# Conversion turns moved from the last batch to batches 2 to 6, and a last V stage with its additions ahead of its statistics

## The chip, the cores and the metric

The kernel runs on one core of a Trainium2 chip. Such a core has engines that run side by side, each with its own queue of instructions: TensorE (PE in the profile, with its weight loader PEld), VectorE (DVE), ScalarE (ACT), GpSimd (POOL) and SyncE (SP), which here issues the DMAs. The metric is the device time of one execution in microseconds. Several runs give a median; one execution was also recorded by the profiler.

## The reference

The program chains three blocks over 8 batches of 576 rows and 512 columns. All sums are kept at float32 accuracy.

```python
# 1. linear attention, 8 heads of 64
q_s = softmax(q, axis=-1); k_s = softmax(k, axis=2)
kv = einsum('bhsd,bhse->bhde', k_s, v)
x = einsum('bhsd,bhde->bhse', q_s, kv)          # then heads side by side: 576 x 512
# 2. gated MLP
h = gelu_tanh(x @ w_in); u, v = h[..., :512], h[..., 512:]
v_n = (v - mean(v)) / sqrt(var(v) + 1e-6) * g_ln
v_s = einsum('ts,bsd->btd', w_sg, v_n) + b_sg[None, :, None]
x = x + (u * v_s) @ w_out
# 3. token mix of rank 32, then channel MLP
u = x + (x.transpose(0, 2, 1) @ U @ V).transpose(0, 2, 1)
out = u + maximum(u @ w_ch1, 0) @ w_ch2         # w_ch1 512 x 2048, w_ch2 2048 x 512
```

## The kernel before

A number is kept as a high and a low part, and a product is three matmuls (high by high, low by high, high by low; `prod`). A tile is 128 rows, so a batch has four tiles of rows and a rest of 64; they are numbered t = 0 to 4.

**Stages of a batch.** The work is a loop over eight batches, numbered 1 to 8 here (0 to 7 in the code). Of each batch the loop runs the V stage (`emit_Vh`: products `pv`, GELU into `ge` on ACT; `stats`: statistics `bst`, `mv` on DVE; `emit_ln`: shift `sh` on DVE, evaluation on ACT, high part `vh` and low part `vl`), then the U stage (`emit_Uh`: products `pu`), the S stage (`emit_S`: products `pS` over the rows, gate `gt` on DVE; `split_G`: `gh` on ACT, `gl` on DVE) and the output stage (`emit_y`: products `py`, addition of `x` into `yt` on DVE). In the last three stages the attention of the next batch runs beside them, and after the output stage `emit_xT` computes that batch's x, transposed: products `px`, copies `xh` and `x` on ACT, low part `xl` on DVE. The first matmuls of the next V stage read `xl`.

**The token mix** of a batch runs inside the next batch's V stage: `emit_yT` transposes (`pt`, then `yh` on ACT and `yl` on DVE), `emit_U` gives `pp` and `pst`, and `emit_PV` gives `pw`, which DVE adds to `yt`; SP then stores `yt` into a buffer in DRAM. `pw`, `pu`, `pS` and `py` share banks, so a product waits until DVE has read the one that had its bank. After batch 8 comes the channel MLP, a Strassen-Winograd scheme of seven products over factors `wd` of the two weight matrices, first in seven steps beside batch 8's token mix, then in groups of steps. Its matmuls are `mm` and `pm`, its weights are loaded as `wu<-wd`.

**Conversion.** Both channel weights arrive as 64-bit floats. A block of them is loaded into `stg`, clamped on POOL (line 171), its exponent is made on ACT (line 177, `f<-stg`), and the fraction is merged in on DVE (lines 183 and 184). Factors are sums of blocks (`f<-f,f`), split into a high part on ACT (`chw<-f`, line 61) and a low part on POOL or DVE (`chw<-f,chw`, line 55), and stored as `wd`. The work is cut into turns. A cycle of eleven turns makes four blocks and seven factors. `turn` begins one item and carries earlier ones a stage on: start after 1 turn, merge after 3, high part after 4, low part after 5, store after 6.

**What sets the order.** PE and DVE carry out the loop in the order in which the program writes it; on ACT, POOL and SP a scheduler orders the instructions of the loop. The places of the turns are written in the table `TURNS[b][stage]`, whose stages are V, U, S, output, and the x products of the next batch. An entry is one slot: `slot` does a turn for each T, and for other letters a single earlier item (P, W, B, S: a split, a store, a bound, a start). `DVE_FACTOR_LOWS` and `DVE_FACTOR_SUMS` say which factors of a batch have low parts and additions on DVE. `STEP_TURNS` and `GROUP_TURNS` do the same for the seven steps and the groups. The slots of the output stage stand ahead of `emit_y` in all batches but the first, where the slot of the first product stands behind it. Most instructions are recorded with the line of a helper: `mm` is line 52, `tt` line 55, `copy` line 61.

Of the kernel before, what the change touches and what calls it, by code (L numbers as in the profile page):

```python
# [22 lines left out]
def fused_kernel(tc, q, k, v, w_in, g_ln, w_sgT, b_sg, w_out, U, V, w_ch1, w_ch2, outT):  # L23
    nc = tc.nc
    B, S, C = q.shape
    P = 128
    H, D = 8, 64
    NT = S // P
# [20 lines left out]
    pe, act, dve, pool, sp = nc.tensor, nc.scalar, nc.vector, nc.gpsimd, nc.sync  # L49
# [421 lines left out]
    def q_max(b, t):  # L471
        if t == 0:
            q_s[b] = tmpp.tile([P, NT + 1, H], F32, tag="qm", name="qm")
        dve.tensor_reduce(
            out=q_s[b][0 : TR[t], t], in_=q3(t), op=ALU.max, axis=mybir.AxisListType.X
        )
# [95 lines left out]
    def behind(eng):  # L572
        return tc.issue_after(last[eng].ins)
# [35 lines left out]
    def emit_Vh(b, t):  # L609
        xh, xl, xr, _ = x_t[b]  # L610
        if b and t == NT:
            pv = ps1.tile([P, F], F32, tag="ps1", name="pv")
        else:
            pv = ps2.tile([P, 1024], F32, tag="big", name="pv")[:, 0:F]
        wv_h, wv_l = wi[1]
        for kc in range(NC):
            if t < NT:
                a, l = xh[:, kc, t * P : (t + 1) * P], xl[:, kc, t * P : (t + 1) * P]
                mm(pv, a, wv_h[:, kc], kc == 0, False)
                mm(pv, a, wv_l[:, kc], False, False)  # L620
                mm(pv, l, wv_h[:, kc], False, kc == NC - 1)
            else:
                a = xr[:, kc].rearrange("p j r -> p (j r)")
                mm(pv, a, wv_h[:, kc], kc == 0, False)
                mm(pv, a, wv_l[:, kc], False, kc == NC - 1)
        if b == 0 and t > 2:
            ge = as_f32(stgp.tile([P, 2, CW], F32R, tag="chw", name="ge", bufs=4)).rearrange("p j n -> p (j n)")
        elif b == B - 1 and t == NT:
            ge = tmpp.tile([P, S], F32, tag="gt", name="ge")[:, 0:F]
        else:  # L630
            ge = tmpp.tile([P, F], F32, tag="ge", name="ge", bufs=3)
        ln[b, t] = ge
        if t < NT:
            act.activation(ge, pv, AF.Gelu_apprx_tanh)
        else:
            copy(ge[0:R], pv[64 : 64 + R])
            tt(dve, ge[0:R], pv[0:R], ge[0:R], ALU.add)
            act.activation(ge[0:R], ge[0:R], AF.Gelu_apprx_tanh)

    def stats(b, t):  # L640
        ge, n = ln[b, t], TR[t]
        bst = tmpp.tile([P, 6], F32, tag="bst", name="bst", bufs=3)
        mv = tmpp.tile([P, 2], F32, tag="mv", name="mv", bufs=3)
        dve.bn_stats(out=bst[0:n], in_=ge[0:n])  # L644
        dve.bn_aggr(out=mv[0:n], in_=bst[0:n])
        dve.tensor_scalar(out=mv[0:n, 1:2], in0=mv[0:n, 1:2], scalar1=1e-6, scalar2=None, op0=ALU.add)
        tt(pool, mv[0:n, 1:2], mv[0:n, 1:2], half[0:n], ALU.pow)
        ln[b, t] = (ge, mv)
# [25 lines left out]
    def emit_ln(b, t):  # L674
        ln_scale(b, t)
        ln_split(b, t)
# [57 lines left out]
    def emit_yT(b, t):  # L734
        n = TR[t]
        if t not in ((2, 3) if b < B - 1 else (1, 2, 3)):
            pt = ps1.tile([P, C], F32, tag="ps1", name="pt1")
        else:
            pt = ps2.tile([P, 1024], F32, tag="big", name="pt1")[:, 0:C]
        for c in range(NC):  # L740
            pe.transpose(pt[0:n, c * P : (c + 1) * P], y_t[b][:, c, t * P : t * P + n], ident)  # L741
        h = wrk.tile([P, C], F32R, tag=f"vh{t}", name=f"yh{t}")
        if t < NT:
            l = wrk.tile([P, C], F32R, tag=f"vl{t}", name=f"yl{t}")
            copy(h, pt)
            low(dve, l, pt, h)
            yn[b, t] = (h, l)
        else:
            copy(h[0:R], pt[0:R])
            low(dve, h[64 : 64 + R], pt[0:R], h[0:R])  # L750
            yn[b, t] = (h,)
# [5 lines left out]
    def emit_U(b, t):  # L757
        if t == 0:
            pu_t[b] = ps1.tile([P, C], F32, tag="ps1", name="pp")
        parts = yn.pop((b, t))  # L760
        w = u_w[:, t].rearrange("p a r -> p (a r)")
        for i, y in enumerate(parts):
            mm(pu_t[b], w, y, t == 0 and i == 0, t == NT and i == len(parts) - 1)
        if t == NT:
            pp = pu_t.pop(b)
            if b < B - 1:
                s = tmpp.tile([P, S], F32R, tag="gt", name="pst")[:, 0:C]
            else:
                s = wrk.tile([P, C], F32R, tag="xr", name="pst")
            copy(s, pp)  # L770
            low(dve, s[3 * RK : P], pp[3 * RK : P], s[3 * RK : P])
            pu_t[b] = s
# [10 lines left out]
    def emit_PV(b, c):  # L783
        s = pu_t[b][:, c * P : (c + 1) * P]
        pw = ps2.tile([P, 2, 512], F32, tag="big", name="pw")
        for j in range(2):
            mm(pw[:, j, 0:HS], s, v_w[:, j * HS : (j + 1) * HS], True, True)
        y = y_t[b][:, c]
        tt(dve, two(y), halves(pw), two(y), ALU.add)
        sp.dma_start(u2d[:, c, :, b * HS : (b + 1) * HS].rearrange("j p n -> p j n"), two(y))  # L790
# [378 lines left out]
    def slot(s):  # L1169
        if isinstance(s, int):  # L1170
            more(s)
            return
        for ch in s:
            if ch == "T":
                more(1)
            elif not gate and at[0] > 0:
                if ch == "L":
                    load_ahead()
                elif {"B": at[0] + 3, "S": at[0] + 1, "M": at[0], "H": at[0], "P": idx["H"] - 1, "W": idx["P"] - 1}[ch] >= idx[ch]:
                    op(ch)  # L1180
# [35 lines left out]
    def in_order(*engines):  # L1216
# [6 lines left out]
    OPS = 4  # L1223
    TURNS = (
# [8 lines left out]
    )  # L1233
    AHEAD = 2
    STEP_TURNS = ('TT', 'TT', 'TT', 'T', 'TTT', 'TTT', 'TTT')
# [16 lines left out]
    FOLDS = ((0, 1, 2, 1, 0), (0, 0, 2, 2, 0))  # L1252
# [71 lines left out]
    for b in range(B):  # L1324
# [10 lines left out]
            fold = k_fold(nxt)  # L1335
        if b > 0:
            load_ahead()
        for t in range(NT + 1):
            emit_Vh(b, t)
            if nxt:  # L1340
                with behind(dve):
                    for t2 in Q_MAX[b > 0][t]:
                        q_max(nxt, t2)
                    for _ in range(FOLDS[b > 0][t]):
                        next(fold)
            if t < NT:
                stats(b, t)
            slot(TURNS[b][0][t])
            if t > 0:
                emit_ln(b, t - 1)  # L1350
            if t == NT:
                stats(b, t)
            if b > 0:
                for t2 in ((2,), (3, 4), (), (), ())[t]:
                    emit_yT(b - 1, t2)
            if t == 2 and b > 0:
                for t2 in range(NT + 1):
                    emit_U(b - 1, t2)
            if b > 0:
                for c in ((), (), (), (0, 1), (2, 3))[t]:  # L1360
                    emit_PV(b - 1, c)

        spread_at = 2 if b else 3
        if nxt:
# [106 lines left out]
        for c in range(NC):  # L1471
            if not nxt:
                for _ in range((3, 3, 2, 0)[c]):
                    next(prep, None)
            if b or c:
                with tc.issue_after(last['s'].ins) if not nxt and c == 0 else contextlib.nullcontext():
                    slot(TURNS[b][3][c])
            emit_y(b, c)
            if b == 0 and c == 0:
                slot(TURNS[b][3][c])  # L1480
            if nxt and 0 < c < 3:
                emit_qT(nxt, 1 + c)
                if c == 2 and b + 2 < B:
                    load_q(b + 2)
# [133 lines left out]
```

## Time and profile before

| | |
|---|---|
| median of 3 runs | 1292.64 us (1290.99 to 1294.96) |
| profiled execution | 1292.16 us |
| its span | 1290.4 us |
| mean granted TensorE clock | 0.989 |
| instructions | 20684 |
| PE busy | 1261.8 us (98%) |
| DVE busy | 969.8 us (75%) |
| ACT busy | 653.3 us (51%) |
| POOL busy | 324.3 us (25%) |
| DMA | 274.17 MB, mean 212 GB/s |

Busy shares are means over the whole span. The span has three parts: some 90 us of preparation with the first batch's attention, the loop to about 613 us, and the channel MLP. Where TensorE is busy nearly all the time, its waits are short and have to be read one by one: by the list of waits, which gives for each kind of instruction what ended its idle time, and by the timeline, whose rows give start, duration, engine, line, operation, tiles and in brackets the idle time ahead with what ended it. A row with x2 stands for two instructions.

### The profile page before, as it was taken

How to read it: one execution, taken by the hardware profiler on the slowest of the kernel's cores; microseconds unless marked ns; L12 is line 12 of the kernel's file. 1: busy time of each engine (PE TensorE's matmuls, PEld its weight loads, DVE VectorE, ACT ScalarE, POOL GpSimd, SP SyncE). 2: the span in 40 equal slices, each digit the busy share in tenths (PEclk: the TensorE clock that was granted, in tenths of full speed). 3: DMA queues.
4: the chain of work that ended last, by engine and by line, in shares of the span. 5: the costliest groups of instructions: out<-in, count | busy, mean ns of one | idle time of the engine just before them, and what ended most of it. 6: DMA issues, size and time to landing. Idle time of an engine off the chain costs nothing.

```text
span 1290.4 us, 20684 instructions
## 1 busy us (share of the span) xinstructions
PE 1261.8 (98%) x7628; PEld 1142.8 (89%) x7628; DVE 969.8 (75%) x1406; ACT 653.3 (51%) x998; POOL 324.3 (25%) x421
## 2 busy tenths in 40 slices
PE   6999999999999999999999999999999999999998
PEld 5798999999998989797887888888888889999998
DVE  6898889797988888788769943597347953694485
ACT  5756667675757576754563512443224522451342
POOL 4734152623333334663630202000200002000000
PEclk8899999999999999999999999999999999999999
DMA  8515161715343352568998676678766788898786
GB/s 271 167 55 167 51 207 51 235 51 167 99 158 117 113 170 76 195 202 284 397 346 295 213 257 235 220 246 281 259 189 224 256 286 303 274 314 302 256 297 212
DMA packets 135909, 274.17 MB, mean 212 GB/s; under 512 B 15232, under 2 KB 56704, under 8 KB 135808
## 3 DMA queue, kind: packets, MB, share of 16 engines
q1 hardware_dynamic: 135808, 272.84, 64.0%
q8 instruction: 61, 1.00, 0.3%
q14 instruction: 40, 0.33, 0.1%
HBM read 224.56 MB, written 48.23 MB: 211 GB/s over the span
## 4 chain that ended last, share of the span: by engine, by line
PE 82%; DVE 8%; DMA 4%; ACT 3%; issue 1%; POOL 1%; SPq 1%; DVEq 0%; POOLq 0%; ACTq 0%
PE mm L52 51%; PE pS L52 8%; PE py L52 6%; PE pv L52 5%; PE pu L52 5%; PE px L52 1%; PE pk L52 1%; PE pt L553 1%; PE pt L741 1%; PE pp L52 1%; DVE bst L644 1%; DVE sh L654 1%; DMA wu<-wd 1%; DVE yt L55 1%; PE pm L52 1%
## 5 line engine op out<-in xcount | busy, mean ns | idle before, releaser
L52 PE MATMUL mm<-oh,wu 128*128 128x512 f32 (+1 forms) x1120 | 320.5, 367 | 1.2 <-DMA wu<-wd 1.2
L52 PE MATMUL mm<-uh,wu 128*128 128x512 f32 (+1 forms) x1064 | 303.4, 366 | 0.0
L52 PEld LDWEIGHTS mm<-oh,wu 128*128 128x128 f32 x1120 | 207.1, 188 | 27.6 <-ACT oh L61 1.6
L52 PEld LDWEIGHTS mm<-uh,wu 128*128 128x128 f32 x1064 | 196.6, 188 | 24.1 <-issue 0.2
L52 PE MATMUL mm<-ol,wu 128*128 128x512 f32 (+1 forms) x560 | 205.5, 367 | 0.0
L61 ACT ACTIVATE oh<-h 128x1024 fp32r<-128x1024 f32 (+1 forms) x140 | 135.2, 973 | 125.3 <-PE mm L52 104.6
L52 PE MATMUL mm<-ul,wu 128*128 128x512 f32 (+1 forms) x532 | 194.7, 366 | 0.0
L55 DVE TENSOR_TENSOR ol<-h,oh 128x1024 fp32r<-128x1024 f32 (+1 forms) x140 | 156.4, 1121 | 40.1 <-ACT oh L61 37.2
L55 POOL TENSOR_TENSOR ust<-ust 128x1024 f32<-128x1024 f32 (+1 forms) x16 | 36.3, 2278 | 384.5 <-DMA ust<-u2d 323.6
L55 DVE TENSOR_TENSOR h<-mm,u 128x1024 f32<-128x1024 f32 (+1 forms) x57 | 63.3, 1111 | 83.8 <-PE mm L52 83.8
L52 PEld LDWEIGHTS mm<-ol,wu 128*128 128x128 f32 x560 | 105.1, 188 | 13.2
L55 DVE TENSOR_TENSOR u<-mm,u 128x1024 f32<-128x1024 f32 (+1 forms) x53 | 58.9, 1111 | 73.2 <-PE mm L52 68.1
L52 PEld LDWEIGHTS mm<-ul,wu 128*128 128x128 f32 x532 | 99.9, 188 | 12.1
L55 POOL TENSOR_TENSOR chw<-f,chw 128x256 fp32r<-128x256 f32 x98 | 80.7, 836 | 97.6 <-ACT chw L61 87.6
L55 DVE TENSOR_TENSOR h<-h,h 128x1024 f32<-128x1024 f32 (+1 forms) x80 | 88.9, 1111 | 0.1
L1102 ACT ACTIVATE h<-mm 128x1024 f32<-128x1024 f32 (+1 forms) x19 | 17.8, 938 | 128.3 <-PE mm L52 128.3
L1093 ACT ACTIVATE h<-h 128x1024 f32<-128x1024 f32 (+1 forms) x60 | 58.1, 969 | 33.6 <-DVE h L55 33.6
L61 ACT ACTIVATE chw<-f 128x256 fp32r<-128x256 f32 x112 | 42.5, 411 | 63.6 <-DVE f L184 30.7
L61 ACT ACTIVATE u<-mm 128x1024 f32<-128x1024 f32 (+1 forms) x24 | 22.5, 936 | 96.3 <-PE mm L52 80.0
L171 POOL TENSOR_SCALAR stg<-stg 128x256 f32<-128x256 f32 (+1 forms) x88 | 44.3, 508 | 91.3 <-DMA stg<-in_w_ch_dram 50.4
L52 PE MATMUL pu<-xh,wih 128*128 128x288 f32 x256 | 57.9, 308 | 1.9 <-ACT wih L61 0.6
L52 PE MATMUL pu<-xh,wil 128*128 128x288 f32 x256 | 56.3, 301 | 1.8 <-DVE wil L55 1.8
(177 smaller groups left out, 2661.8 us busy)
## 6 DMA issues: line engine op xcount, KB each, us to landing
wu<-wd SPq DMA_DIRECT2D x280, 512.0 KB, 4.4
wd<-chw SPq DMA_DIRECT2D x112, 256.0 KB, 3.5
stg<-in_w_ch_dram SPq DMA_DIRECT2D x64, 256.0 KB, 3.5
u2d<-yt SPq DMA_DIRECT2D x32, 288.0 KB, 2.3
vt<-in_v_dram SPq DMA_DIRECT2D x32, 256.0 KB, 6.9
qt<-in_q_dram SPq DMA_DIRECT2D x7, 1024.0 KB, 8.2
kt<-in_k_dram SPq DMA_DIRECT2D x7, 1024.0 KB, 6.4
res<-u2d SPq DMA_DIRECT2D x12, 512.0 KB, 5.8
```

What stands on the lines that cost most here:

```text
L52: pe.matmul(out, lhsT, rhs, start=first, stop=last, skip_group_check=onto)
L55: return eng.tensor_tensor(out=out, in0=a, in1=b, op=op)
L61: return act.activation(out, src, AF.Copy)
L171: eng.tensor_scalar(out=hi, in0=hi, scalar1=F64_MOST, scalar2=-F64_MOST, op0=ALU.min, op1=ALU.max)
L553: pe.transpose(pt[:, t * P : (t + 1) * P], qt[:, t, c * P : (c + 1) * P], ident)
L644: dve.bn_stats(out=bst[0:n], in_=ge[0:n])
L654: dve.scalar_tensor_tensor(out=shift[0:n], in0=mv[0:n, 0:1], scalar=-1.0, in1=mv[0:n, 1:2], op0=ALU.mult, op1=ALU.mult)
L741: pe.transpose(pt[0:n, c * P : (c + 1) * P], y_t[b][:, c, t * P : t * P + n], ident)
L1093: act.activation(h, h, AF.Relu)
L1102: act.activation(h_out(j, 11, n), bank, AF.Relu)
```

## The change

It changes the table in the rows of batches 2 to 6 and 8, the place of the first output slot, and the order of the last V stage.

- Output stage: two turns more in each of batches 2 to 5, three more in batch 6. Batch 8 loses eleven: its U stage goes from seven to two, its S stage from five to none, its output stage from seven to six; in its V stage the turns of the fourth and fifth slot are put together into the fifth. The number of all turns, `STEP_TURNS` and `GROUP_TURNS` stay.
- In batches 2 to 7 the slot of the first output product now stands behind `emit_y(b, 0)`, as it did in the first.
- In batch 8 a loop of its own writes the V stage: `emit_U` and `emit_PV` ahead of `stats`, the LayerNorm of tile 2 and 3 ahead of the slot, `emit_yT` last.

```diff
-        (('T', '', '', '', ''), ..., ('TT', 'TTTT', 'TTW', ''), ...
+        (('T', '', '', '', ''), ..., ('TT', 'TTTT', 'TTTW', 'T'), ...
...
-        (('TTT', 'TT', 'TT', 'T', 'TT'), ('TT', 'T', 'T', 'TTT'), ('TT', 'T', 'TT', ''), ('TTT', 'TT', 'PT', 'T')),
+        (('TTT', 'TT', 'TT', '', 'TTT'), ('T', 'T', '', ''), ('', '', '', ''), ('TT', 'TT', 'PT', 'T')),
...
+        else:
+            for t in range(NT + 1):
+                emit_Vh(b, t)
+                if t == 2:
+                    for t2 in range(NT + 1):
+                        emit_U(b - 1, t2)
+                for c in ((), (), (), (0, 1), (2, 3))[t]:
+                    emit_PV(b - 1, c)
                 stats(b, t)
-            slot(TURNS[b][0][t])
-            if t > 0:
-                emit_ln(b, t - 1)
-            if t == NT:
-                stats(b, t)
-            if b > 0:
+                if t >= NT - 1:
+                    emit_ln(b, t - 1)
+                slot(TURNS[b][0][t])
+                if 0 < t < NT - 1:
+                    emit_ln(b, t - 1)
                 for t2 in ((2,), (3, 4), (), (), ())[t]:
                     emit_yT(b - 1, t2)
...
-            if b or c:
+            if c or not nxt:
                 with tc.issue_after(last['s'].ins) if not nxt and c == 0 else contextlib.nullcontext():
                     slot(TURNS[b][3][c])
             emit_y(b, c)
-            if b == 0 and c == 0:
+            if nxt and c == 0:
                 slot(TURNS[b][3][c])
```

DVE in the last V stage, from the additions of the second matrix of the mix on; before, `pst` and both pairs of `yt` stand behind the statistics `bst` of a tile:

```order
L55 TENSOR_TENSOR pst<-pp,pst 32x512
L644 BN_STATS bst<-ge 128x6
L645 BN_AGGR mv<-bst 128x2
L646 TENSOR_SCALAR mv<-mv 128x1
L183 TENSOR_SCALAR f_6710<-f_6710 128x256
L184 SCALAR_TENSOR_TENSOR f_6710<-stg,f_6710 128x256
L654 SCALAR_TENSOR_TENSOR sh<-mv 128x1
L55 TENSOR_TENSOR yt<-pw,yt 128x576 x2
L55 TENSOR_TENSOR ge<-pv,ge 64x512
L654 SCALAR_TENSOR_TENSOR sh<-mv 128x1
L644 BN_STATS bst<-ge 64x6
```

The same stretch in the changed kernel, behind the statistics of one tile more and with the first pair of `yt` in it:

```order
L55 TENSOR_TENSOR pst<-pp,pst 32x512
L644 BN_STATS bst<-ge 128x6
L645 BN_AGGR mv<-bst 128x2
L646 TENSOR_SCALAR mv<-mv 128x1
L183 TENSOR_SCALAR f_6707<-f_6707 128x256
L184 SCALAR_TENSOR_TENSOR f_6707<-stg,f_6707 128x256
L183 TENSOR_SCALAR f_6716<-f_6716 128x256
L184 SCALAR_TENSOR_TENSOR f_6716<-stg,f_6716 128x256
L654 SCALAR_TENSOR_TENSOR sh<-mv 128x1
L55 TENSOR_TENSOR yt<-pw,yt 128x576 x2
L644 BN_STATS bst<-ge 128x6
```

The `bst` behind `pst` is tile 2's after the change and tile 3's before it; the first pair `yt` stands ahead of tile 3's statistics after the change and behind them before it.

DVE at the end of batch 4's V stage, where the fifth slot has one turn in both kernels; `yt` are additions of the mix, `ge` the rest tile's products, and marked rows are new:

```order
 L55 TENSOR_TENSOR yt<-pw,yt 128x576 x2
 L55 TENSOR_TENSOR ge<-pv,ge 64x512
+L55 TENSOR_TENSOR chw<-f_2943,chw 128x256
+L183 TENSOR_SCALAR f_3056<-f_3056 128x256
+L184 SCALAR_TENSOR_TENSOR f_3056<-stg,f_3056 128x256
 L654 SCALAR_TENSOR_TENSOR sh<-mv 128x1
 L644 BN_STATS bst<-ge 64x6
```

The turn there is four turns later in the cycle than before, and so brings a low part and a merge.

ACT between batch 3 and batch 4, at the copies of the transposed attention products (`xh`, `x` from `px`), before:

```order
L61 ACTIVATE xh<-px 128x576
L61 ACTIVATE x_3070<-px 128x576
L61 ACTIVATE yh_3096<-pt_3091 128x512
L61 ACTIVATE chw<-f_2952 128x256
L61 ACTIVATE xh<-px 128x576 x2
L61 ACTIVATE x_3070<-px 128x576
L61 ACTIVATE yh_3127<-pt_3122 128x512
L177 ACTIVATE f_3598<-stg 128x256
L61 ACTIVATE x_3070<-px 128x576
```

And after, from the same copy `x`, the second of the four, on:

```order
L61 ACTIVATE x_3096<-px 128x576
L61 ACTIVATE chw<-f_2952 128x256
L61 ACTIVATE chw<-f_2943 128x256
L177 ACTIVATE f_3064<-stg 128x256
L61 ACTIVATE yh_3122<-pt_3117 128x512
L61 ACTIVATE xh<-px 128x576
L61 ACTIVATE chw<-f_2934 128x256
L61 ACTIVATE xh<-px 128x576
L61 ACTIVATE x_3096<-px 128x576
L177 ACTIVATE f_3347<-stg 128x256
L61 ACTIVATE yh_3153<-pt_3148 128x512
L61 ACTIVATE x_3096<-px 128x576
```

Between the second and the third `x` one instruction of the conversion stood before, and four stand now.

## Rows read from the trace of the kernel before

**Rows 1.** The page: busy time, share of the span and instructions of each engine.

```profile
PE 1261.8 (98%) x7628; PEld 1142.8 (89%) x7628; DVE 969.8 (75%) x1406; ACT 653.3 (51%) x998; POOL 324.3 (25%) x421
```

**Rows 2.** Windows between S stages: length, busy (x) per engine, clock, DMA share, GB/s.

```profile
143.95:212.62 68.67, 68.45 (x532) 64.58 (x531) 58.16 (x107) 43.64 (x71) 24.56 (x35) 1.00 0.39 122
212.62:281.29 68.67, 68.45 (x531) 64.57 (x531) 58.72 (x109) 45.35 (x77) 28.47 (x41) 1.00 0.44 141
...
487.29:557.70 70.41, 68.21 (x523) 63.67 (x523) 57.34 (x110) 47.52 (x90) 40.50 (x52) 1.00 0.45 152
557.70:613.19 55.49, 53.76 (x330) 48.20 (x330) 48.74 (x75) 24.57 (x51) 25.29 (x29) 1.00 0.76 248
613.19:700.00 86.81, 85.63 (x379) 70.59 (x378) 65.99 (x76) 45.23 (x70) 35.34 (x49) 1.00 0.97 354
```

**Rows 3.** Waits of PE, 500 to 700: us in total, times, longest.

```profile
PE pw L52 <- DVE yt L55: 1.7, 2, 1.3
PE mm L52 <- DMA wu<-wd: 1.2, 1, 1.2
PE pm L52 <- ACT h L1102: 0.8, 1, 0.8
PE py L52 <- DVE gl L55: 0.5, 1, 0.5
PE pu L52 <- DVE yt L55: 0.5, 1, 0.5
PE pw L52 <- DVE pst L55: 0.3, 1, 0.3
```

**Rows 4.** Timeline of PE in the last V stage.

```profile
543.27 0.53 PE L52 MATMUL pw<-v_w,pst 128*128 128x288 f32 x2 [1.29 <-DVE yt L55]
```

**Rows 5.** Waits of PE's weight loader, 110 to 520.

```profile
PEld pu L52 <- DVE yt L55: 1.8, 6, 0.3
PEld px L52 <- DVE xl L55: 1.7, 6, 0.3
```

**Rows 6.** Timeline of DVE and POOL in the last V stage.

```profile
538.30 0.70 DVE L55 TENSOR_TENSOR pst<-pp,pst 32x512 fp32r<-32x512 f32 x1
...
540.96 1.39 DVE L184 SCALAR_TENSOR_TENSOR f<-stg,f 128x256 uint32<-128x256 uint32 x1
...
542.46 1.42 DVE L55 TENSOR_TENSOR yt<-pw,yt 128x576 f32<-128x576 f32 x2
...
540.69 1.38 POOL L55 TENSOR_TENSOR vl<-ge,vh 128x512 fp32r<-128x512 f32 x1
```

**Rows 7.** Timeline of DVE in an output stage: low part, shift, or.

```profile
296.13 0.42 DVE L55 TENSOR_TENSOR chw<-f,chw 128x256 fp32r<-128x256 f32 x1
296.47 0.29 DVE L183 TENSOR_SCALAR f<-f 128x256 uint32<-128x256 uint32 x1
296.79 0.42 DVE L184 SCALAR_TENSOR_TENSOR f<-stg,f 128x256 uint32<-128x256 uint32 x1
```

**Rows 8.** Timeline of ACT, DVE and PE between batches 3 and 4.

```profile
248.55 0.45 ACT L61 ACTIVATE chw<-f 128x256 fp32r<-128x256 f32 x1
248.86 1.23 ACT L61 ACTIVATE xh<-px 128x576 fp32r<-128x576 f32 x2
249.92 0.71 ACT L61 ACTIVATE x<-px 128x576 f32<-128x576 f32 x1
...
250.67 0.76 DVE L55 TENSOR_TENSOR xl<-px,xh 128x576 fp32r<-128x576 f32 x1 [0.33 <-ACT x L61]
...
251.87 0.40 PE L52 MATMUL pv<-wih,xl 128*128 128x512 f32 x1
```

**Rows 9.** End of batch 4's V stage: timeline of DVE, chain of waits.

```profile
270.22 1.40 DVE L55 TENSOR_TENSOR yt<-pw,yt 128x576 f32<-128x576 f32 x2
...
271.01 3.45 PE pu L52 x24
```

**Rows 10.** Timeline of ACT in an output stage.

```profile
235.22 0.42 ACT L61 ACTIVATE chw<-f 128x256 fp32r<-128x256 f32 x1 [1.39 <-DMA wd<-chw]
```

More of the change, by code (lines that the diff above doesn't have):

```diff
@@ L1337, in fused_kernel @@
             load_ahead()
[L1338 to L1346, printed above, removed]
-                stats(b, t)
-            slot(TURNS[b][0][t])
-            if t > 0:
-                emit_ln(b, t - 1)
-            if t == NT:
-                stats(b, t)
-            if b > 0:
+        if nxt:
+            for t in range(NT + 1):
+                emit_Vh(b, t)
+                if nxt:
+                    with behind(dve):
+                        for t2 in Q_MAX[b > 0][t]:
+                            q_max(nxt, t2)
+                        for _ in range(FOLDS[b > 0][t]):
+                            next(fold)
+                if t < NT:
+                    stats(b, t)
+                slot(TURNS[b][0][t])
+                if t > 0:
+                    emit_ln(b, t - 1)
+                if t == NT:
+                    stats(b, t)
+                if b > 0:
+                    for t2 in ((2,), (3, 4), (), (), ())[t]:
+                        emit_yT(b - 1, t2)
+                if t == 2 and b > 0:
+                    for t2 in range(NT + 1):
+                        emit_U(b - 1, t2)
+                if b > 0:
+                    for c in ((), (), (), (0, 1), (2, 3))[t]:
+                        emit_PV(b - 1, c)
+        else:
+            for t in range(NT + 1):
+                emit_Vh(b, t)
+                if t == 2:
+                    for t2 in range(NT + 1):
+                        emit_U(b - 1, t2)
+                for c in ((), (), (), (0, 1), (2, 3))[t]:
+                    emit_PV(b - 1, c)
+                stats(b, t)
+                if t >= NT - 1:
+                    emit_ln(b, t - 1)
+                slot(TURNS[b][0][t])
+                if 0 < t < NT - 1:
+                    emit_ln(b, t - 1)
                 for t2 in ((2,), (3, 4), (), (), ())[t]:
                     emit_yT(b - 1, t2)
[L1356 to L1361, printed above, removed]
         spread_at = 2 if b else 3
```

10 rows, old and new, of the table TURNS are left out of this document.

## The prediction

> **What bounds the kernel now.** I read the busy times of the page first, then the windows by batch, then what TensorE waited for, and last the timelines round the places that the change touches. TensorE is busy for 1261.8 of 1290.4 us [rows 1]. A gain can therefore come only from the 28.6 us in which it is not, and a loss only where another engine makes it late. The windows cut the program where the S stage of a batch begins. The one from batch 2's S stage takes 68.67 us with 68.45 us of matmul in it, the next the same, although the first carries 35 and the second 41 POOL instructions [rows 2]; five periods are of this kind, those whose output stages get turns. So the turns that already lie there are paid for with nothing but idle time of other engines. The period with the last V and U stage takes 70.41 us with 68.21 us of matmul, 1.74 us more than the others. The last S and output stage take 55.49 us, 53.76 us of them matmul, and the stretch to 700 has 85.63 of 86.81 us, with the DMA engines at 0.97 [rows 2]. What is to be had lies here, between 487 and 700 us.
>
> The waits in that part have names [rows 3]: 1.7 us for additions `yt` in front of the token-mix products `pw`, 0.5 us for `yt` in front of the U products `pu`, 0.3 us for `pst`, 0.5 us for `gl`, 0.8 us for a ReLU on ACT and 1.2 us for a weight load. The larger piece of the 1.7 us, 1.29 us, lies in the last V stage, ahead of the third and fourth `pw` [rows 4]. In all the batches from 2 on, TensorE's weight loader waits once each for `yt` in front of `pu` and for `xl` in front of `px`, 0.3 us at most [rows 5]: operands that come with no slack. A microsecond more ahead of one of those is a microsecond of the total.
>
> **The last batch: what the change removes.** DVE does `pst` at 538.30, then statistics and a merge whose or is stretched to 1.39 us, and only at 542.46 the additions that free the banks of `pw` [rows 6]. The new order puts `pst` ahead of the second tile's statistics, and each pair of additions ahead of the statistics beside it; the held merge between is gone from there. So the 1.29 us go, since `pw` had long been ready for them; the 0.3 us go, since `pst` comes earlier by three small instructions and two merges; and the 0.5 us in front of `pu` go, because the second pair of additions no longer stands behind statistics that wait for ACT's last GELU. Gain 1.29 + 0.3 + 0.5 = 2.1 us. What is late next is the LayerNorm evaluation, whose reader, the S stage, comes a whole U stage later, so nothing. Bounds: 1.3 us, if the small waits stay, to 2.5 us, if the rest of the 1.7 goes too.
>
> The last batch also loses ten turns in its U and S stages. No wait of TensorE stands there [rows 3], so nothing comes back. The 0.5 us for `gl` stay: S products, gate and split stand in a row there, and the change leaves that chain. The ReLU and the load (0.8 and 1.2 us) lie behind the turns of the step table, which is unchanged; with fewer POOL reads in front DVE may be earlier. I take 0.3 us, between 0 and 2.5.
>
> **Batches 2 to 6: what the change adds.** Eleven turns go into the stages of output products, two in each of batches 2 to 5 and three in batch 6: four clamps on POOL, four exponents on ACT, four merges of two instructions on DVE, seven copies on ACT, seven low parts and four additions on DVE or POOL, and seven stores. From one start to the next DVE pays 0.34 us for a low part and 0.32 us for the shift of a merge, and 0.42 us at most for its or [rows 7]; ACT pays 0.31 us for a copy (248.55 to 248.86) [rows 8], and I use that for an exponent of the same shape too. That is 4 us of each engine in 343 us. The only question is in front of which of the slackless places they land.
>
> First place, the end of the V stage of batch 4, where a slot that has one turn in both kernels gets other content: a low part and a merge between `ge` and the last additions. They stand in front of the `yt` at 270.22; the second U group starts at 271.01 in the chain, right behind the first of these two additions [rows 9]. Cost 0.34 + 0.32 + 0.34 = 1.0 us; 0 if they only fill a hold that another DVE instruction has there now; 2.0 if the or is held as at 540.96, which adds 1.39 - 0.42. I take 1.0, since this DVE stretch has no idle time.
>
> Second place, the transposed attention products at the end of each batch: there the copies of ACT stand in one queue with those of the conversion. At the end of batch 3 the last `xl` on DVE waits for the copy `x` that starts at 249.92, begins at 250.67, ends 0.76 us later, and the matmul that reads it starts at 251.87 [rows 8]. Slack 251.87 - 251.43 = 0.44 us, with one `chw` copy in front; without one it would be 0.44 + 0.31 = 0.75 us. The new order has four conversion instructions in front of that `x` in place of one: three more are 0.93 us, less 0.44 is 0.5 us lost. At the end of batch 4 there are three where there was none: 0.93 - 0.75 = 0.2 us. At the end of batch 2 there are four where there was none, two of them ahead of the first `xh`, where ACT idles for products; the other two are 0.62 us and fit, unless the first two come late from their merge: 0.3 us, from 0 to 0.6. The ends of batches 5 and 6 get one or two more each: 0.2 us together, from 0 to 0.6. Sum 1.2 us, from 0.4 to 2.3.
>
> Third place, the additions `yt` of the output stage: in batches 4 and 6 one more low part of 0.34 us on DVE lies ahead of one of them. I take 0.2 us, from 0 to 0.7. The first slot behind its addition moves merges from in front of `yt` to behind it; no wait of TensorE stands at that addition [rows 3, 5], so nothing.
>
> **A rule against the change.** Beside a `vl` on POOL of 1.38 us, begun at 540.69, the or at 540.96 took 1.39 us [rows 6]; by itself it takes 0.42 us [rows 7]. The Trainium skill, "SBUF — State Buffer", section "Who interferes with whom", says that a DVE instruction with two SBUF inputs contends with a POOL instruction that reads SBUF, and that the port is locked for a whole instruction. By that rule the trace agrees, and since each added turn brings about one POOL instruction into periods in which DVE is already full, holds would multiply.
>
> **Sum.** The profiled execution took 1292.16 us, the span of 1290.4 and 1.76 around it. Minus 2.1 minus 0.3, plus 1.0 + 1.2 + 0.2, is 0.0: 1292.2 us. The median of the three runs is 0.48 above the profiled one, so a median is forecast at 1292.6 us, with a range of its own of 1291 to 1294.5. This kernel's timing can tell 0.3%, 3.9 us, from no change, so 1288.8 to 1296.5 us counts as the same.
>
> **Rivals.**
> A. The added turns hide wholly, as those before do: equal periods with 35 and 41 POOL instructions speak for it [rows 2], the counted slack of 0.44 us and the chain that passes through `yt` against it [rows 8, 9]. Only the gains remain: 1292.6 - 2.4 = 1290.2 us. Chance 0.24; this is still the same.
> B. The stage after the last batch gets quicker as well: the ReLU's 0.8, the load's 1.2 and 0.3 us more, on top of 2.1: 4.4 us, 1288.2 us. For it speaks that loads wait for stores that DVE, POOL and ACT make, eleven turns of which are done earlier; against it that the DMA engines are at 0.97 there and the turns of the steps unchanged. Chance 0.08, the only faster case.
> C. Slower: ACT's queue blocks. A copy `chw` waits until the store that reads its buffer has landed; at 235.22 ACT stood 1.39 us for that [rows 10]. With two or three more copies in each output stage and the same few buffers, that wait would move in front of the `xh` and `x` copies, which TensorE reads within 0.44 to 0.75 us. It decides as soon as it is longer than that slack. At all five transitions: 5 x 1.39 = 7.0 us in place of the 1.2 that I count, plus 5.8: 1298.4 us; at three of them 1295.6. Against it: the one such wait in the trace stands where TensorE had slack. Chance 0.07.
> D. Slower by holds: if at each of the five transitions one merge or low part is held by POOL in front of a slackless place, each loses 1.39 - 0.42 = 0.97 us: 4.9 us more, 1297.5 us. Against it: the periods with 35 and 41 POOL instructions have one length. Chance 0.04.
>
> **Numbers.** Forecast 0.57, A 0.24, B 0.08, C 0.07, D 0.04. Faster by over 0.3%: 0.08 (B). Within: 0.81 (forecast and A). Slower: 0.11 (C and D). The range has to hold A at 1290.2 and the milder form of C at 1295.6; with the bounds of the sum it is 1289.5 to 1296.5 us.
>
> **What will show it.** In the list of waits of the changed kernel the 1.29, 0.5 and 0.3 us of the last V stage are gone; if the 1.29 stays, the first step is wrong. The period with the last V stage shrinks to about 68.5 us, that of batch 3 to 4 and of batch 4 to 5 grow by 1.0 to 1.5 us together with a wait at `pu` for `yt` and one at `pv` or `px` for `xl`; the others grow by 0.1 to 0.4. If all five stay at 68.67, A is right; if ACT's `chw` waits for a store between `xh` copies, C is; if merges of 1.3 us and more stand in front of `yt` or `xl`, D is. The 0.5, 0.8 and 1.2 us should stand as before; if they go, B is.

## The result, and the profile after

The changed kernel takes 1307.64 us in the median of six runs (1301.86 to 1312.72), the kernel before 1292.84 us (1290.99 to 1296.79): ratio 1.0109, 95% interval 1.0079 to 1.0138. It is slower by some 14 us, where 1292.6 was forecast with a range up to 1296.5. The profiled execution took 1308.93 us with a span of 1307.1 us, 16.7 us more than before.

TensorE's list of waits between 100 and 500 us, in the changed kernel (us in total, times, longest). The same stretch had less than 1 us of such waits before. Three of these waits, 1.02 us for `yt` and 0.97 and 0.57 us for `xl`, lie ahead of the first stage that the change touches.

```profile
PE pv L52 <- ACT xh L61: 6.7, 5, 2.1
PE pv L52 <- DVE xl L55: 2.4, 4, 0.7
PE px L52 <- DVE xl L55: 1.9, 3, 1.0
PE pu L52 <- DVE yt L55: 1.1, 1, 1.1
PE px L52 <- DVE yt L55: 1.0, 1, 1.0
PE pw L52 <- DVE yt L55: 0.8, 1, 0.8
```

Five waits of `pv` for the copy `xh` on ACT make up half of it; five is the number of batches with added turns. The windows from one S stage to the next, answering to [rows 2]:

```profile
147.02:221.04 74.02, 70.39 (x532) 65.31 (x531) 61.51 (x111) 46.37 (x80) 31.46 (x46) 0.98 0.42 138
221.04:292.32 71.28, 68.80 (x530) 64.24 (x529) 58.51 (x110) 43.83 (x72) 21.48 (x32) 1.00 0.39 124
292.32:366.19 73.87, 71.17 (x533) 65.64 (x532) 61.94 (x114) 47.14 (x82) 28.76 (x39) 0.98 0.41 134
366.19:437.33 71.14, 69.01 (x531) 64.35 (x531) 59.34 (x114) 44.43 (x72) 21.21 (x31) 1.00 0.40 125
437.33:508.06 70.73, 69.24 (x532) 64.34 (x531) 60.62 (x114) 46.48 (x79) 26.31 (x37) 1.00 0.43 136
508.06:575.27 67.21, 67.16 (x523) 63.67 (x523) 54.10 (x105) 44.84 (x83) 37.70 (x49) 1.00 0.46 152
```

Against 68.67 us the five periods are longer by 5.35, 2.61, 5.20, 2.47 and 2.06, in sum 17.7 us. The last one is shorter than before by 70.41 - 67.21 = 3.2 us. The first S stage here begins 3.1 us later than before (147.02 against 143.95), though nothing in the program is changed ahead of it; over the kernels profiled for this case that moment lies between 141.9 and 147.6. What follows 575.27 gives back 0.9. These four make up the 16.7 us.

ACT at the end of batch 2 (timeline: start, duration, engine, line, operation, tiles, in brackets the idle time ahead and what ended it):

```profile
183.06 0.62 ACT L61 ACTIVATE yh<-pt 128x512 fp32r<-128x512 f32 x1
186.98 0.42 ACT L61 ACTIVATE chw<-f 128x256 fp32r<-128x256 f32 x1 [3.31 <-DMA wd<-chw]
187.30 0.63 ACT L61 ACTIVATE xh<-px 128x576 fp32r<-128x576 f32 x1
187.83 0.41 ACT L61 ACTIVATE chw<-f 128x256 fp32r<-128x256 f32 x1
188.14 0.64 ACT L61 ACTIVATE xh<-px 128x576 fp32r<-128x576 f32 x1
```

A conversion copy stands for 3.31 us in front of two copies `xh` that could have run (their products `px` had ended by 184.1), since its buffer is still being read by a store. SP's issues and the chain of waits (cut) show where the store stood and how long it took:

```profile
176.06 0.32 SPq L384 DMA_DIRECT2D wd<-chw  x1
176.47 0.39 SPq L133 DMA_DIRECT2D qt<-in_q_dram  x1
176.96 1.15 SPq L384 DMA_DIRECT2D wd<-chw  x2
178.20 0.51 SPq L134 DMA_DIRECT2D qt<-in_q_dram  x1
178.80 3.42 SPq L213 DMA_DIRECT2D stg<-in_w_ch_dram  x3
```

```profile
176.96 9.94 DMA wd<-chw
...
186.98 0.42 ACT chw L61
```

The store was issued right behind the load of q (1 MB) and took 9.94 us to land; the median of all stores `wd` is 4.2 us in this kernel and 3.5 us in the one before. TensorE is out of work for over 2 us, and comes back at its lower clock level (1.2 GHz). First TensorE's timeline, then windows of 2 us (length, busy times, then the granted clock, DMA share, GB/s):

```profile
185.46 0.39 PE L52 MATMUL pv<-wih,xl 128*128 128x512 f32 x1
187.99 0.67 PE L52 MATMUL pv<-wih,xh 128*128 128x512 f32 x1 [2.13 <-ACT xh L61]
188.45 0.63 PE L52 MATMUL pv<-wil,xh 128*128 128x512 f32 x1
```

```profile
188.00:190.00 2.00, 2.00 (x5) 1.19 (x5) 1.37 (x2) 2.00 (x5) 1.36 (x4) 0.54 0.82 248
190.00:192.00 2.00, 2.00 (x8) 1.61 (x8) 2.00 (x5) 1.97 (x3) 2.00 (x6) 0.61 1.03 370
192.00:194.00 2.00, 2.00 (x10) 1.59 (x10) 1.93 (x5) 1.05 (x3) 1.75 (x4) 1.00 1.08 352
```

Over some 3.5 us a matmul takes 0.63 in place of 0.39 us. The same happens at the end of batch 4, after waits of 1.93 and 0.50 us. These are the two periods that lose over 5 us. ACT waits for stores between or just ahead of the copies from `px` at all five ends: 3.31, 1.00, 2.79, 2.15 and 1.60 us, 10.9 in sum. The stores waited for took 9.94, 5.17, 5.18, 8.29 and 6.57 us; all five were issued behind the load of q, by 0.5 to 4.4 us. ACT's list of waits between 100 and 520 us, before and after:

```profile
ACT chw L61 <- DMA wd<-chw: 1.4, 1, 1.4
ACT chw L61 <- DMA wd<-chw: 11.0, 6, 3.3
```

### The profile page after: what moved, and what is told of

It reads as the page before. It is cut to its first block, busy times and chain, and to the rows that moved or that the text cites. A ratio compares the mean times of both kernels' runs of the same rounds, so it can differ in the third digit from the quotient of the medians.

```text
span 1307.1 us, 20678 instructions
## 1 busy us (share of the span) xinstructions
PE 1264.4 (97%) x7628; PEld 1140.1 (87%) x7628; DVE 967.1 (74%) x1407; ACT 654.5 (50%) x998; POOL 321.8 (25%) x420
## 4 chain that ended last, share of the span: by engine, by line
PE 73%; DVE 12%; DMA 7%; ACT 3%; issue 2%; POOL 2%; SPq 1%; DVEq 0%; POOLq 0%; ACTq 0%
PE mm L52 51%; PE pS L52 7%; PE pv L52 5%; PE pu L52 5%; DMA wd<-chw 3%; PE py L52 2%; DMA stg<-in_w_ch_dram 2%; PE pp L52 1%; DVE f L183 1%; DVE f L184 1%; DMA wu<-wd 1%; DVE yt L55 1%; DVE bst L644 1%; PE pt L741 1%; DVE sh L654 1%
## 5 line engine op out<-in xcount | busy, mean ns | idle before, releaser
L55 POOL TENSOR_TENSOR chw<-f,chw 128x256 fp32r<-128x256 f32 x95 | 76.7, 819 | 93.5 <-ACT chw L61 93.3
L61 ACT ACTIVATE chw<-f 128x256 fp32r<-128x256 f32 x112 | 42.7, 412 | 70.7 <-DVE f L184 27.0
L171 POOL TENSOR_SCALAR stg<-stg 128x256 f32<-128x256 f32 (+1 forms) x88 | 47.1, 541 | 99.3 <-DMA stg<-in_w_ch_dram 47.7
L52 PE MATMUL pv<-wih,xh 128*128 128x512 f32 x128 | 53.7, 419 | 6.7 <-ACT xh L61 6.7
```

The source lines that it names most:

```text
L52: pe.matmul(out, lhsT, rhs, start=first, stop=last, skip_group_check=onto)
L55: return eng.tensor_tensor(out=out, in0=a, in1=b, op=op)
L61: return act.activation(out, src, AF.Copy)
L171: eng.tensor_scalar(out=hi, in0=hi, scalar1=F64_MOST, scalar2=-F64_MOST, op0=ALU.min, op1=ALU.max)
```

## The experiments

Theory 1: the loss comes from stores that land late, so that a buffer of `chw` comes free late and a copy `chw<-f`, in ACT's order, holds what stands behind it. Theory 2: it comes from the number of instructions that the turns bring. Theory 3: from the new V stage. All ratios are against the kernel before, timed beside the version.

**The V stage alone.** Only the loop of batch 8 is taken over, with the table of before.

```diff
+        else:
+            for t in range(NT + 1):
...
+                for c in ((), (), (), (0, 1), (2, 3))[t]:
+                    emit_PV(b - 1, c)
                 stats(b, t)
```

> Kernel before with only the new order of the last V stage; table of turns and first output slot as before. Theory 1 (the loss comes from ACT's queue standing in front of a conversion copy until a store has landed, between the batches) and theory 2 (the loss comes from the mere number of instructions added on ACT and DVE in batches 2 to 6) both expect the periods of batches 2 to 6 at 68.67 us, the waits of 1.29, 0.5 and 0.3 us in the last V stage gone, and 1292.8 - 2.1 = 1290.7 us, ratio 0.998. If the new V stage carries the loss (theory 3), 1300 us or more.

Measured: 1297.54 us, ratio 1.0033 (1.0021 to 1.0045); a miss for all theories. The waits in the V stage do go: from 489.81 to the last S stage at 556.9 it is 67.1 us in place of 70.41. Part of the gain is lost ahead of it: the period of batch 6, whose turns are those of before, takes 70.4 us, with a store wait of 1.91 us on ACT and 0.76 us of TensorE for `xh` behind it. The rest is lost right behind the V stage. ACT and TensorE in the S and output stage of batch 8:

```profile
576.12 0.63 ACT L61 ACTIVATE uh<-us 128x512 fp32r<-128x512 f32 x1 [3.77 <-DMA us<-u2d]
576.65 0.67 ACT L61 ACTIVATE gh<-gt 128x576 fp32r<-128x576 f32 x1
```

```profile
572.90 0.53 PE L52 MATMUL py<-gl,wo_h 128*128 128x288 f32 x2 [0.70 <-DVE gl L55]
574.49 0.54 PE L52 MATMUL py<-gl,wo_h 128*128 128x288 f32 x2 [0.53 <-DVE gl L55]
577.38 0.53 PE L52 MATMUL py<-gh,wo_h 128*128 128x288 f32 x2 [2.08 <-ACT gh L61]
```

It is ACT's queue again, this time behind a load: `uh` waits 3.77 us for the data that the channel MLP needs, and `gh` stands behind it. The granted clock falls to 0.67 and then 0.50 in the windows after that. In the full change, where turns behind it go as well, TensorE has no such wait for `gh`; that these turns are the reason was not tested by itself.

**The turns alone.** New table and first slot, batch 8's V stage written as before.

```diff
-        else:
-            for t in range(NT + 1):
...
+            if b > 0:
+                for c in ((), (), (), (0, 1), (2, 3))[t]:
+                    emit_PV(b - 1, c)
```

> Changed kernel with the V stage of the last batch written as before: new table of turns and first slot behind its addition stay. Theories 1 and 2: the five periods stay 2 to 5 us longer, store waits of ACT as in the changed kernel, and 1307.6 + 2 = about 1309 us (1304 to 1313). Theory 3: below 1297 us.

Measured: 1309.6 us, ratio 1.0128 (1.011 to 1.0146), with 12.2 us of ACT's waits for stores. The loss is in the turns; theory 3 falls. Beside them the new V stage shortens the last period from 69.0 to 67.2 us, a difference that the two medians cannot tell. Without it the period is still 1.4 us shorter than before.

**The first slot alone.**

```diff
-            if b or c:
+            if c or not nxt:
...
-            if b == 0 and c == 0:
+            if nxt and c == 0:
```

> Kernel before with only the first output slot of batches 2 to 7 behind its addition. All theories: no wait of TensorE stands there, no change beyond 1.5 us, 1291 to 1294 us.

Measured: 1291.98 us, ratio 0.9989 (0.9973 to 1.0004): no change that can be told, as expected.

**Five buffers.**

```diff
-    bb = cst.tile([P, S], F32, name="bb")
+    bb = None
...
-    chw = [((stgp, 4),), 0]
+    chw = [((stgp, 5),), 0]
```

> Changed kernel with five instead of four buffers for converted factors. To make room the bias of the gate is left out (its addition reads another tile of the same shape, its load at the start is gone). Theory 1: a copy finds a free buffer while a late store is on its way, so ACT's waits for stores between the batches fall from 10.9 us in sum to under 3, the five periods to 68.7 to 69.7 us, no drop of the granted clock there, and the time to 1291 to 1297 us, 1294 say. Theory 2: the same number of instructions, so the same periods (70.7 to 74.0) and 1305 to 1310 us.

Measured: 1301.06 us, ratio 1.0054 (1.0035 to 1.0072). Theory 2 is out as the whole cause, since the turns and their instructions are the same and 6.6 us are gone; but more is left than theory 1 gave. In ACT's list 5.2 us for stores are left, the longest 2.3. The periods of batches 2 and 4 are still 4.6 and 4.1 us longer than before, and in batch 4 the granted clock falls to 0.53 after waits of 1.09 and 0.60 us; theory 1 had expected neither.

```profile
ACT chw L61 <- DMA wd<-chw: 5.2, 3, 2.3
```

**A small load of q.**

```diff
-            sp.dma_start(qt[:, t : t + step, :], src)
+            sp.dma_start(qt[0 : (16 if b > 1 else P), t : t + step, :], src[0 : (16 if b > 1 else P)])
```

> Changed kernel in which the loads of q for batches 3 to 8 move an eighth of their rows (128 KB of 1 MB; the rest of q keeps old values, so the attention of those batches is computed from other data). The load's place in the queue stays. Theory 1 with the q load as what makes the stores late: the store at the end of batch 2, 9.94 us from issue to landing, takes under 6 us, waits of ACT for stores fall under 4 us in sum, time 1292 to 1299. Theory 1 without it (the stores and block loads delay one another): store waits stay above 7 us, time 1301 or more. Theory 2: 1304 to 1310 us.

Measured: 1296.51 us, ratio 1.0027 (1.0016 to 1.0038): 11 of the 15 us are gone with seven eighths of the bytes of one load per batch, as theory 1 with the q load had it. The two stores behind that load at the end of batch 2 land in 3.6 us, in place of 9.9 (medians of two). ACT's waits for stores were expected under 4 and are 4.1 us; none of them holds an `xh` for which TensorE waits. What is left are waits for DVE:

```profile
PE pv L52 <- DVE xl L55: 1.7, 4, 0.6
PE px L52 <- DVE xl L55: 1.4, 3, 0.7
PE pw L52 <- DVE pst L55: 1.3, 1, 1.3
PE pu L52 <- DVE yt L55: 1.1, 1, 1.1
```

The five periods are still 7.9 us longer in sum than before, of the 17.7 in the changed kernel. Of what is left, the 1.3 us at `pst` stand behind a store wait of 2.15 us (193.98) in the V stage.

**The load of q on another queue.** ACT issues it, with all its bytes; the same in the kernel before as a control.

```diff
-            sp.dma_start(qt[:, t : t + step, :], src)
+            (act if b > 1 else sp).dma_start(qt[:, t : t + step, :], src)
```

> Changed kernel in which ACT issues the loads of q for batches 3 to 8, all of their bytes, in place of SP. If the stores are late because they stand behind the q load in SP's own DMA queue (theory 1, queue): stores land in under 6 us, the store waits of ACT fall under 4 us in sum, time 1293 to 1300. If they are late because the q load takes the bandwidth of the DMA engines (theory 1, bandwidth): store waits stay at 8 us or more and the time at 1304 or more; ACT's issues cost it some 1 us a batch besides.

> Kernel before with the loads of q for batches 3 to 8 issued by ACT. No store wait stands on the path there, so all theories expect no change beyond 2 us: 1291 to 1295 us. It is the control for the run with the changed kernel, and shows what ACT's issues cost.

Measured: 1302.55 us, ratio 1.0082 (1.0053 to 1.0111), between the two forms of the theory; the control 1293.6 us, 1.001 (0.9997 to 1.0024), no change. In the chain of the changed kernel with q on ACT, the store at the end of batch 2 still takes 8.64 us:

```profile
175.42 8.64 DMA wd<-chw
```

So for this store its place behind the load in one queue is the smaller part; that the load's megabyte moves at that moment is the larger. Of the time, the other queue gave back 5 us and the small load 11. That the bandwidth of the DMA engines is the limit is not shown: in the changed kernel their share in windows of 2 us from 176 on is 0.61, 0.64, 0.82, 1.02 and 0.99, so they were not full over all of the store's time. In the control, with the turns of before, the period of batch 6 takes 70.7 us, with a store wait of 2.17 us ahead of an `xh`. As with the V stage alone, such a wait comes there without an added turn in some executions, so the 2.06 us of the changed kernel's batch 6 cannot be put down to its added turns alone.

**Three buffers in the kernel before.**

```diff
-    chw = [((stgp, 4),), 0]
+    chw = [((stgp, 3),), 0]
```

> Kernel before with three instead of four buffers for converted factors. Theory 1: the wait of the changed kernel can be made in the kernel before by taking a buffer away: store waits of ACT rise from 3 us in sum to 8 or more, some of them between the px copies, time 1296 to 1306 us. Theory 2: the number of instructions stays, so 1291 to 1294 us.

Measured: 1300.87 us, ratio 1.0062 (1.004 to 1.0085), with 12.0 us of waits for stores in fifteen pieces. The time is as theory 1 had it, but not for its reason: the periods of batches 4 to 6 stay at 68.7 us, since these waits lie in the output stages, ahead of copies that TensorE doesn't need yet. Of the 10.8 us by which the span is longer, 8.1 lie behind the start of the last S stage, where among others `mm` waits 2.0 us for `u` and 1.1 us for `h` on ACT. In these periods a store wait costs nothing; what stands behind it decides.

**Two turns.** The kernel before with the change at the end of batch 2 alone.

```diff
-        ... ('T', 'T', 'TTT', 'TT'), ('TT', 'TTTT', 'TTW', ''), ...
-        ... ('', 'TT', 'TT', 'TT'), ('TTT', 'TTTT', 'TT', 'T'), ...
+        ... ('T', 'T', 'TTT', 'TT'), ('TT', 'TTTT', 'TTTW', 'T'), ...
+        ... ('', 'TT', 'TT', 'TT'), ('T', 'TTTT', 'TT', 'T'), ...
```

> Kernel before with two turns moved from batch 3's output stage to the end of batch 2's, as the change does there; last batch as before. Only at the end of batch 2 does ACT's order get chw copies between the px copies, and at the end of batch 3 one moves. Theory 1: the store wait of some 3 us and the drop of the granted clock come there and nowhere else, the period of batch 2 is 72 to 74 us and the other four 68.7 to 69.3, time 1295 to 1299 us. Theory 2: no turn is added over batches 2 and 3 together, so 1291 to 1294 us.

Measured: 1297.27 us, ratio 1.0036 (1.0021 to 1.0051). The windows of batches 2, 3 and 4, and ACT at the end of batch 2:

```profile
142.87:215.99 73.12, 69.27 (x532) 64.35 (x531) 60.97 (x111) 46.15 (x80) 30.94 (x46) 1.00 0.44 139
215.99:284.73 68.74, 68.46 (x532) 64.57 (x531) 57.03 (x105) 42.60 (x68) 20.34 (x30) 1.00 0.36 114
284.73:353.41 68.68, 68.44 (x531) 64.58 (x531) 58.83 (x111) 44.70 (x76) 20.75 (x30) 1.00 0.40 125
```

```profile
182.58 0.42 ACT L61 ACTIVATE chw<-f 128x256 fp32r<-128x256 f32 x1 [3.08 <-DMA wd<-chw]
```

With no turn added over batches 2 and 3 together, the end of batch 2 loses 4.45 us and the others nothing. The store waited for was again issued right behind the load of q and took 9.72 us. TensorE waits 1.91 us here and its clock doesn't fall; theory 1 had expected that fall too, and missed it.

**The turns behind the copies from px.** The added ones move to the end of the stage of x products.

```diff
-        ... ('TT', 'TTTT', 'TTTW', 'T'), ('', '', '', '', '')),
+        ... ('TT', 'TTTT', 'TTW', ''), ('', '', '', '', 'TT')),
```

> Changed kernel with the same number of turns in each of batches 2 to 6, but the eleven added ones at the end of the stage of x products, behind the copies from px, where in four of the five ends no chw copy stands between the copies on ACT any longer (at the end of batch 3 three still do). Theory 1 (place: a chw copy between the px copies stands in front of them until a store has landed): no store wait between the px copies at four ends, periods 68.7 to 69.7 us there and about 71 at the end of batch 3, time 1290 to 1296 us. Theory 2 (number of added instructions): the same instructions are there, so 1304 to 1310 us.

Measured: 1301.76 us, ratio 1.008 (1.0062 to 1.0098); a miss for both. The copies from `px` are free at the end of batch 2, but the loss has moved on into the next V stage, where the additions of the token mix have no slack either:

```profile
196.78 0.53 PE L52 MATMUL pw<-v_w,pst 128*128 128x288 f32 x2 [0.97 <-ACT ge L634]
199.38 0.54 PE L52 MATMUL pw<-v_w,pst 128*128 128x288 f32 x2 [2.06 <-DVE yt L55]
```

No store wait of ACT stands ahead of these two. POOL's clamp waits 2.78 us for the load of a block (191.78), `vl` stands behind it in POOL's order, and ACT's `ge` waits 2.42 us for `vl` (196.13). Elsewhere ACT's waits for stores are still 9.0 us in sum, two of them, 1.10 and 2.41 us, ahead of an `xh` at the ends of batches 3 and 5; only the first was expected.

**A whole cycle in one batch.** All eleven turns in batch 2, or in batch 4; ACT's order between the copies from `px` is that of before at the other ends.

```diff
-        ... ('T', 'T', 'TTT', 'TT'), ('TT', 'TTTT', 'TTTW', 'T'), ...
+        ... ('TT', 'TT', 'TTTT', 'TTT'), ('TTTTT', 'TTTTTT', 'TTTTW', ''), ...
```

> Changed kernel, last batch and first slot as there, but all eleven added turns in batch 2 (one more in each S slot, three, two and two more in the first output slots) and none in batches 3 to 6. Eleven turns are one whole cycle, so ACT's order between the px copies is that of the kernel before at all five ends. Theory 1 (place): no store wait between the px copies beyond those of the kernel before, periods from batch 3's S stage on 68.7 us and the last 67.2; batch 2 alone may lose up to 4 us to crowding in its S and output stages. Time 1289 to 1294 us. Theory 2 (number of added instructions): 11 turns cost as much wherever they stand, 1303 us or more.

> The same with the eleven turns in batch 4, whose period has 21.02 us of POOL, the fewest. ACT's order at the ends of the other batches is that of the kernel before; at the end of batch 4 a chw copy stands ahead of the first xh. Theory 1: time 1289 to 1294 us, with batch 4 losing up to 3 us if that copy waits for its store. Theory 2: 1303 us or more.

Measured: 1302.87 us, ratio 1.0076 (1.0053 to 1.0099), and 1300.54 us, 1.0058 (1.0037 to 1.0078). Half right: the other periods are back at 68.7 us and the last at 67.2 to 67.8, so little is lost where ACT's order is as before. But the batch that takes the cycle loses 14.5 us in one case and 11.2 in the other, of which 4.4 and 3.9 us are matmul time at the lower clock. With the cycle in batch 2, TensorE waits twice for an addition `yt` (in the list of waits):

```profile
PE px L52 <- DVE yt L55: 6.5, 2, 5.9
PE pt L553 <- DVE yt L55: 4.3, 1, 4.3
```

The longer wait, at 187.80, stands behind a store: ACT waits 5.45 us for it in the output stage (184.61) and DVE's merge 6.81 us behind that. The 4.3 us, at 176.40, come ahead of this store wait. There DVE's merges wait 2.63 and 2.15 us for exponents on ACT, ACT waits 1.86 us for an addition on POOL, and POOL 2.61 us for the load of a block. With the cycle in batch 4 the two longest waits have no store ahead of them either; ACT's only wait for one in that loop stage, 3.18 us, comes later (325.21). DVE's low parts wait 2.11 and 3.14 us for additions `f` on POOL, which ahead of the first works without a pause from 295.4 to 305.4. DVE and TensorE there:

```profile
304.78 0.93 DVE L55 TENSOR_TENSOR chw<-f,chw 128x256 fp32r<-128x256 f32 x1 [2.11 <-POOL f L55]
307.09 0.85 PE L52 MATMUL py<-gh,wo_h 128*128 128x288 f32 x2 [4.13 <-DVE ql L55]
```

So 4.3 of the 10.2 us of waits in the first case, and 6.2 of 7.3 in the second, come without a store wait of ACT, behind conversion work that waits for POOL, for ACT or for a load.

**Seven and four.** The cycle split over two batches, so that no `chw` copy stands between the copies from `px` at either end.

```diff
-        ... ('', 'TT', 'TT', 'TT'), ('TTT', 'TTTT', 'TTT', 'TT'), ...
-        ... ('', 'TT', 'TTT', 'TTT'), ('TT', 'TTT', 'TT', 'T'), ...
+        ... ('T', 'TTT', 'TTT', 'TT'), ('TTTTT', 'TTTTT', 'TTT', 'T'), ...
+        ... ('T', 'TTT', 'TTT', 'TTT'), ('TTT', 'TTTT', 'T', ''), ...
```

> Changed kernel, last batch and first slot as there, with seven of the eleven turns in batch 3 and four in batch 4 (one to each of some S slots, the rest in the first output slots), so that no chw copy stands between the px copies at the ends of these two batches. Theory 1 (a copy that waits for a store costs only where copies of px stand behind it): no store wait between px copies, periods of batches 3 and 4 at 68.7 to 70 us, the others at 68.7, the last at 67.2; 1289 to 1293 us, faster than both kernels or even. Theory 2 (batches 2 to 6 have no room for the added instructions at all, seven turns crowd one batch as eleven did): periods of batches 3 and 4 longer by 8 us or more together, 1298 us or more.

> The same with four turns in batch 4 and seven in batch 5; ACT's order between the px copies is free of chw at both ends. Theory 1: 1289 to 1293 us. Theory 2: 1298 us or more.

Measured: 1307.88 us, ratio 1.0107 (1.0092 to 1.0122), and 1302.12 us, 1.0059 (1.0045 to 1.0074). Theory 1 in the form "only the place between the px copies costs" falls. The chain in the first, ACT, DVE and TensorE in the output stage of batch 3:

```profile
250.10 0.42 ACT L61 ACTIVATE chw<-f 128x256 fp32r<-128x256 f32 x1 [3.63 <-DMA wd<-chw]
```

```profile
250.55 0.99 DVE L55 TENSOR_TENSOR chw<-f,chw 128x256 fp32r<-128x256 f32 x1 [8.20 <-ACT chw L61]
252.12 0.75 DVE L55 TENSOR_TENSOR yt<-py,x 128x576 f32<-128x576 f32 x1
```

```profile
253.01 0.82 PE L52 MATMUL px<-qh,kh 128*128 128x288 f32 x2 [8.01 <-DVE yt L55]
```

A low part on DVE waits 8.20 us for its high part on ACT, which waits 2.48 us for an addition on POOL (245.43) and then 3.63 us for a buffer; `yt` stands behind it in DVE's order, and `px` needs the bank that `yt` frees. In the second version TensorE waits 2.02 us at 312.76 for a `yt` with no store wait of ACT in its way: DVE works through conversion instructions from 306.2 to 311.9 with one pause of 0.59 us.

Theory 1 holds for the ends of the batches in the changed kernel, and in a wider form for the crowded batches. A conversion instruction may wait for a store, for the load of a block or for another engine's stage. Wherever it waits, from the output stage to the next V stage, something soon stands behind it for which TensorE has no slack. Theory 2 falls as the cause of the whole loss, but not altogether: in the batches that take seven or eleven turns the instructions of the conversion themselves fill DVE and POOL. How much of the 7.9 us left with the small load is of that kind was not measured. No version here beats the kernel before.

## Why the prediction was wrong

**The last batch.** Expected: 2.1 us from the three waits, and little else. The 1.29, 0.5 and 0.3 us are gone as said, and the period fell to 67.21 us, 3.2 us shorter, where 68.5 was written: TensorE's idle time there is down to 0.05 us, so all of the 2.2 us went, and a microsecond of matmul time beside it. That the turns which leave the U and S stages give nothing back was wrong: with the V stage of before they shorten the period by 1.4 us, and without their leaving the new V stage made the kernel slower by 0.33%.

**The end of batch 4's V stage.** Expected 1.0 us at `pu` for `yt`, answering to [rows 9]. Measured 1.07:

```profile
282.20 0.53 PE L52 MATMUL pu<-xh,wih 128*128 128x288 f32 x2 [1.07 <-DVE yt L55]
```

The sum of instruction times held: from `ge` to this `yt` DVE takes 3.78 us (277.63 to 281.41) in place of 2.78 (267.44 to 270.22). Its parts are others than written: the new low part takes 1.53 us beside `vl` on POOL, and the shift `sh`, which took 1.26 us in that place before, now takes 0.15.

**The transposed attention products.** This is the step that failed: "The new order has four conversion instructions in front of that `x` in place of one: three more are 0.93 us, less 0.44 is 0.5 us lost." It priced a copy by its running time, 0.31 us, and found 1.2 us over the five ends. A copy also needs a buffer, and the wait for it was 1.0 to 3.3 us at each. The single such wait in the loop of before [rows 10] showed the mechanism with 1.39 us, at a place with slack; it said that the store, not the copy, sets the price. With seven eighths of one load's bytes gone, 11 us went away. What stayed was still over the forecast: the five periods are 7.9 us longer, where 1.0 + 1.2 + 0.2 = 2.4 was counted, so the sum of instruction times was too small apart from the late stores too. Which waits make up the difference is known only in part.

**Rival C** named this mechanism and got a chance of 0.07. Its price, 5 x 1.39 us, was too small: the waits sum to 10.9 us, waits for `xl` behind them come on top, and twice the lower clock after TensorE had stood still. The argument against it, that the wait of before stood where there was slack, was the one to mistrust, since the change moves just such copies to where there is none.

**Rival D and the rule of the port.** Held instructions on DVE do occur, and two stand on the way to a wait of TensorE: the low part of 1.53 us above, where the hold only moved from one instruction to another, and a shift of 0.85 us ahead of the 0.81 us at `pw` (204.84). They are small beside the waits for stores. **Third place and first slot:** 0.2 us was taken for the additions of the output stage; no wait of TensorE for one of them stands behind 147 us. The first slot cost nothing, as said. **Tail:** the waits for `gl` and the ReLU stand with 0.5 and 0.7 us, the load's is 0.5 in place of 1.2 us, and the gain of 0.9 us behind the last S stage is in the range of 0 to 2.5 that was given.

## What to carry to other kernels

A step moved to another stage takes along what it waits for. Before pricing it by its duration, list its buffers and what frees them, and read from the trace how long that takes at the new place, with the transfers that run there. An instruction that may wait for a transfer should not stand in an in-order queue ahead of one that the bounding engine reads within a microsecond. And an equal period under different loads shows slack only for the work that was in it, in the order in which it stood.

## What was not expected of the hardware

A store of 256 KB took 9.94 us from issue to landing while a 1 MB load and three 256 KB loads were under way, against a median of 4.2 us over the run, and 8.64 us with the large load on another engine's queue. The granted clock was at the lower level for some 3.5 us after TensorE had stood still for 2.13 us (0.54 in a window of 2 us), and after waits of 1.93 and 0.50 us (0.50). With five buffers it fell after waits of 1.09 and 0.60 us (0.53), and with two turns it did not fall after 1.91 and 0.42 us. The length of the wait alone does not say whether it falls.
